# Block-causal attention and two feed-forward layers on one core: the first part as one list ordered at build time, with two-bank PSUM tiles and quartered tail scores

## The chip, the cores and the metric

The kernel runs on one core of a Trainium2 chip. The metric is the device time of one execution in microseconds, the lower the better. Before the change three runs gave 958.18, 959.80 and 960.07, a median of 959.8 us.

## The reference

Attention has 4 batches of 8 heads, 576 positions of 64 numbers, and a mask by blocks of 64: a query sees all keys of its own block and of earlier ones. Two feed-forward layers follow, each 512 to 2048 to 512 over 2304 tokens. All is float32.

```
scores = (q @ k.T) / sqrt(64);  scores = where(pos_q // 64 >= pos_k // 64, scores, -1e9)
attn   = exp(scores - max);  attn = attn / (sum(attn) + 1e-9);  x = attn @ v      # heads side by side
h = x @ w_in1;   g = where(h >= 1, h, where(h <= -1, 0, (h + 1)**2 / 4));  x = g @ w_out1
h = x @ w_in2;   g = h * cos(h);                                           out = g @ w_out2
```

## The kernel before

**Attention** goes over 16 pairs of heads (4 batches, 4 pairs each). The two heads of a pair lie in the upper and lower 64 partitions of `Q` and `K`. The 576 queries are four blocks of 128 and a tail of 64 (`LAST`, `TAIL`). For each pair: transposes bring K and Q from their loads (`prep`, L472; copies L478, L480, L485); score matmuls fill PSUM (`scores`, L505), the block scores of the two heads in two row halves of the array, with a short matmul `mk_k, mk_q` that adds the mask; VectorE takes the negated row maximum (L533), ScalarE the exponential with the row sum (L544), VectorE adds 1e-9 and takes the reciprocal (L562, L565; for tails L539, L553, L557), GpSimd multiplies (L573). `p_trans` transposes the probabilities (L600) and ScalarE or VectorE copies them out of PSUM (L616, L614); `pv` multiplies by V, the two heads in two column halves (L631), and ScalarE copies the result to `xs` (L642 to L645), which goes to DRAM (`x1d`).

The work of a pair has two groups, blocks 0, 1 and the tail (`GROUPS[0]`) and blocks 2, 3. The tail queries of both heads stand in one 128-column operand padded with zeros (`Q[:, S - TAIL:S + TAIL]`), so that a full-array matmul gives both heads' tail scores, the keys in two halves of 288; two half maxima, two half sums and two exponentials are joined afterwards. PSUM has eight tiles of one bank.

The order is a program's: `attention` yields after each piece, and `at(d, fn)` puts a follow-up (a reduce, an exponential, a copy) `d` pieces later. Weight conversion is called in the same way. A weight arrives as 64-bit words; ScalarE and GpSimd turn the two halves into fields (L267, L269, L273), VectorE joins them (L280, L284), and the float is rounded to a high part (L309 to L312) and a low rest (L251). Fourteen of the 32 halves of layer 1's weights are converted during attention, the others in layer 1.

**Layer 1** has 4.5 blocks of 512 tokens with 16 steps of 128 hidden columns. A step is `mm1` (12 matmuls, L755), the activation (L772, L775, L778, then L248 for the high part and L251 for the low part) and two steps later `mm2` (12 matmuls, L801). Each product is high by high, high by low and low by high. `first_split` splits the input of the first block while attention runs, right behind the scores of pairs 1 to 4. Layer 2's weights are combined during layer 1 (`w_combine`, L343 to L362) and stored to DRAM from GpSimd's queue (L374).

**Layer 2** (L970, L1062) is a seven-product scheme. Its operations stand in a list, `Plan`, which simulates four queues at build time with a cost for each operation and emits the instructions in that order.

The rule of `at`, and the calls that follow a score matmul:

```
at(1, top); at(2, exp)
if u == (3,) and 1 <= n <= NK: at(3, lambda: first_split(n - 1))
if u != (2,): at(5, norm)
```

Of the kernel before, what the change touches and what calls it, by code (L numbers as in the profile page):

```python
# [9 lines left out]
F32 = mybir.dt.float32  # L10
# [17 lines left out]

class Plan:

    def __init__(self):
        self.ops, self.wrote, self.read = [], {}, {}

    def add(self, eng, cost, reads, writes, fn):
        n, pre = len(self.ops), set()
        for r in reads:
            if r in self.wrote:
                pre.add(self.wrote[r])
            self.read.setdefault(r, []).append(n)
        for w in writes:  # L40
            pre.update(self.read.pop(w, ()))
            if w in self.wrote:
                pre.add(self.wrote[w])
            self.wrote[w] = n
        pre.discard(n)
        self.ops.append((eng, cost, pre, fn))

    def run(self):
# [3 lines left out]
        for i, (eng, cost, pre, fn) in enumerate(self.ops):  # L52
            for p in pre:
                post[p].append(i)
            if eng == "P":
# [4 lines left out]
        for i in reversed(range(n)):  # L60
            left[i] = self.ops[i][1] + max([left[j] + (0.0 if chain[j] == i else self.LAG) for j in post[i]], default=0.0)
        need = [len(op[2]) + (chain[i] is not None) for i, op in enumerate(self.ops)]
        ready_at, free = [0.0] * n, {"P": 0.0, "V": 0.0, "A": 0.0, "S": 0.0}
        ready = {e: [i for i in range(n) if self.ops[i][0] == e and need[i] == 0] for e in free}
        done = 0
        while done < n:
            best = None
            for e, r in ready.items():
                if r:
                    t = max(free[e], min(ready_at[i] for i in r))  # L70
                    if best is None or t < best[0]:
                        best = t, e
            t, e = best
            i = min((i for i in ready[e] if ready_at[i] <= t), key=lambda i: (-left[i], i))
            ready[e].remove(i)
            self.ops[i][3]()
            end = t + self.ops[i][1]
            free[e] = t if e == "S" else end
            for j in post[i]:
                need[j] -= 1  # L80
                ready_at[j] = max(ready_at[j], end + (0.0 if chain[j] == i else self.LAG))
                if need[j] == 0:
                    ready[self.ops[j][0]].append(j)
            done += 1

    LAG = 0.15
# [3 lines left out]
def attn_moe_moe_kernel(ctx: ExitStack, tc: tile.TileContext, q, k, v, w_in1, w_out1, w_in2, w_out2, out):  # L90
# [9 lines left out]
    NI = (S + 127) // 128  # L100
    TAIL = S - 128 * (NI - 1)
    LAST = NI - 1
    scale = 1.0 / float(D) ** 0.5

    const = ctx.enter_context(tc.tile_pool(name="const", bufs=1))
    dram = ctx.enter_context(tc.tile_pool(name="dram", bufs=1, space=DRAM))
    KB = 1024
# [32 lines left out]


# [14 lines left out]
    def warm():  # L156

        z = M.e.tile([128, 512], F32, name="warm", tag="ea")[:, 0:64]
        nc.vector.memset(z, 0.0)
        M.z = z.bitcast(BF16)  # L160
        M.zo = M.h[0].tile([128, 512], F32, name="h", tag="h")
        idle(36)

    def idle(n):
        for _ in range(n):
            tc.keep_in_program_order(nc.tensor.matmul(  # L166
                out=M.zo[:, 0:128], lhsT=M.z, rhs=M.z, start=True, stop=True, skip_group_check=True
            ))

    def consts():  # L170
        make_identity(nc, ident)

# [16 lines left out]


    now = [0]
    due = {}

    def at(d, fn):
        if d == 0:
            fn()
        else:
            due.setdefault(now[0] + d, []).append(fn)

    def tick():  # L200
        now[0] += 1
        for fn in due.pop(now[0], ()):
            fn()

    def flush():
        while due:
            tick()

    class Pools:
        pass  # L210

    M = Pools()
    M.wb = None
    M.two = []


    w_raw, w_in, w_out, rnds, raw_slot = {}, {}, {}, {}, {}
    srcs = {1: (w_in1, w_out1), 2: (w_in2, w_out2)}

    def home(f, which):  # L220
        arena, n = (M.A1, f) if f < NWA else (M.W2, f - NWA)
        return Slots(arena, (2 * n + which) * 4 * KB, 4 * KB)

    def w_load(layer, f, which):

        def load(slot, f):
            a = slot.tile([128, 2 * DM], I32)
            w = srcs[layer][which].bitcast(I32)
            if which == 0:
                dst = a.rearrange("p (k f) -> p k f", k=NK)  # L230
                src = w[:, f * 256:(f + 1) * 256].rearrange("(k p) f -> p k f", p=128)
            else:
                dst, src = a, w[f * 128:(f + 1) * 128, :]
            with tc.issue_after(P.loaded.ins):
                nc.sync.dma_start(out=dst, in_=src)
            return a

        if layer == 1:
            raw_slot[f, which] = M.raws.pop(0)
            w_raw[layer, f, which] = load(raw_slot[f, which], f)  # L240
        else:
            assert M.two.pop()
            w_raw[layer, f, which] = [
                load(Slots(M.F1, (8 + 4 * i) * KB, 4 * KB), f + NF // 2 * i) for i in range(2)
            ]

    def rounded(hi, raw):
        return nc.gpsimd.tensor_scalar(out=hi, in0=raw, scalar1=1.0, scalar2=1.0, op0=ALU.mult, op1=ALU.mult)  # L248

# [3 lines left out]
    def wait_for(i, other):  # L253
        tc.add_manual_dep(
# [1040 lines left out]
```

## Time and profile before

| | |
|---|---|
| median of 3 runs | 959.8 us (958.18 to 960.07) |
| profiled execution | 959.37 us, of which the span of the trace is 957.5 us |
| granted TensorE clock | 0.996 of full speed in the mean |
| busy | TensorE 943.0 us (98%), VectorE 703.3 (73%), ScalarE 542.2 (57%), GpSimd 349.2 (36%) |
| chain that ended last | TensorE 76%, VectorE 10%, ScalarE 8%, issue 2%, GpSimd 2%, DMA 1% |

In the trace PE is TensorE's matmuls and PEld its weight loads, DVE is VectorE, ACT ScalarE, POOL GpSimd, SP the queue that issues DMAs. Ends of matmuls are modelled, so that neighbours overlap; the distance from one start to the next is safer than a duration. A float32 matmul leaves two records. A row of busy time by stage has the stretch, its length, then busy time and instructions of PE, PEld, DVE, ACT and POOL, then the granted clock, DMA's share and GB/s. A row of a group of instructions has engine, operation, shapes and count, then busy time and the mean of one in ns, then the idle time in front of it and who ended it. A row of a timeline or of the chain has its start and its length in us.

### The profile page before, as it was taken

To read this page: it belongs to the slowest core of one execution; us is meant where nothing else is said; L and a number is where in the kernel's file an instruction comes from. 1 tells how busy PE (TensorE), PEld (TensorE's weight loads), DVE (VectorE), ACT (ScalarE), POOL (GpSimd) and SP (SyncE) were. 2 spreads that over 40 slices of the span, in tenths; PEclk is the share of its full clock that TensorE was granted. 3 is DMA by queue.
4 is the path that set the end of the run, shared out by engine and by line. 5 is a ranking of instruction groups with operands and counts; after the bars stand their busy time and mean duration, and the time that the engine had idled before them with its cause. 6 is when DMAs were issued, how large, how long until landed. Compare 5 with 4: busy or idle time off the path is not lost.

```text
span 957.5 us, 17583 instructions
## 1 busy us (share of the span) xinstructions
PE 943.0 (98%) x6524; PEld 843.4 (88%) x6524; DVE 703.3 (73%) x1078; ACT 542.2 (57%) x1067; POOL 349.2 (36%) x437
## 2 busy tenths in 40 slices
PE   8999999999999999999999999999999999999997
PEld 7777888778888888988888888999999999999997
DVE  5788887776766576787687622899977899578883
ACT  5778888865555555554455322568515684166641
POOL 2567776777755656576666110000000000000000
PEclk9999999999999999999999999999999999999999
DMA  5656555345347456646456450877798777877771
GB/s 113 188 146 162 158 146 144 94 157 185 101 144 252 155 190 238 205 176 226 170 180 242 140 190 19 268 253 252 258 311 300 253 245 260 276 275 252 250 261 52
DMA packets 131588, 188.84 MB, mean 197 GB/s; under 512 B 63408, under 2 KB 96688, under 8 KB 131504
## 3 DMA queue, kind: packets, MB, share of 16 engines
q1 hardware_dynamic: 123824, 158.36, 51.4%
q0 software_dynamic: 7680, 29.36, 8.3%
q8 instruction: 52, 0.85, 0.4%
q14 instruction: 32, 0.26, 0.1%
HBM read 144.18 MB, written 43.52 MB: 196 GB/s over the span
## 4 chain that ended last, share of the span: by engine, by line
PE 76%; DVE 10%; ACT 8%; issue 2%; POOL 2%; DMA 1%; SPq 0%; ACTq 0%; DVEq 0%; POOLq 0%
PE q L1062 19%; PE a L801 18%; PE q L970 18%; PE h L755 18%; ACT P L544 7%; DVE m L533 2%; DVE f L284 1%; DVE d L562 1%; DVE f L280 1%; DVE PT L614 1%; POOL m L251 1%; DVE g L251 1%; PE s L505 1%; DVE f L343 1%; PE h L166 1%
## 5 line engine op out<-in xcount | busy, mean ns | idle before, releaser
L1062 PE MATMUL q<-m 128*128 128x256 f32 x1512 | 181.9, 283 | 0.0
L1062 PEld LDWEIGHTS q<-m 128*128 128x128 f32 x1512 | 181.8, 192 | 0.0
L970 PE MATMUL q<-m 128*128 128x384 f32 x1008 | 175.2, 334 | 0.0
L970 PEld LDWEIGHTS q<-m 128*128 128x128 f32 x1008 | 174.7, 188 | 0.1
L801 PE MATMUL a<-g,m 128*128 128x512 f32 (+1 forms) x780 | 172.3, 368 | 1.3 <-DVE g L251 1.3
L801 PEld LDWEIGHTS a<-g,m 128*128 128x128 f32 x780 | 136.9, 188 | 26.9 <-DVE g L251 2.6
L251 DVE TENSOR_TENSOR g<-f,g 128x512 fp32r<-128x512 f32 (+1 forms) x80 | 70.8, 885 | 54.8 <-POOL g L248 54.7
L573 POOL TENSOR_SCALAR P<-P,r 128x576 f32<-128x576 f32 (+2 forms) x144 | 91.5, 652 | 51.1 <-DVE r L565 32.0
L544 ACT ACTIVATE P<-s,m 128x288 f32<-128x288 f32 (+4 forms) x160 | 81.4, 524 | 36.5 <-DVE m L539 28.1
L755 PE MATMUL h<-m 128*128 128x512 f32 (+1 forms) x468 | 98.7, 359 | 0.0
L772 ACT ACTIVATE f<-h,half 128x512 f32<-128x512 f32 (+1 forms) x80 | 51.2, 640 | 81.5 <-PE h L755 73.3
L248 POOL TENSOR_SCALAR g<-f 128x512 fp32r<-128x512 f32 (+1 forms) x80 | 54.9, 687 | 109.0 <-DVE f L778 104.3
L755 PEld LDWEIGHTS h<-m 128*128 128x128 f32 x468 | 79.0, 191 | 13.3 <-issue 0.8
L778 DVE SCALAR_TENSOR_TENSOR f<-f,h 128x512 f32<-128x512 f32 (+1 forms) x80 | 50.3, 628 | 49.9 <-ACT f L775 49.9
L755 PE MATMUL h<-x,m 128*128 128x512 f32 x312 | 75.9, 389 | 0.0
L533 DVE TENSOR_REDUCE m<-s 128x1 f32<-128x288 f32 (+4 forms) x160 | 67.2, 473 | 3.4 <-PE s L505 3.4
L505 PE MATMUL s<-K,Q 128*128 128x288 f32 (+4 forms) x320 | 67.6, 469 | 1.5 <-ACT P L544 1.2
L755 PEld LDWEIGHTS h<-x,m 128*128 128x128 f32 x312 | 58.3, 188 | 11.9
L280 DVE SCALAR_TENSOR_TENSOR f<-f 128x512 uint32<-128x512 uint32 x64 | 45.1, 725 | 19.4 <-ACT f L273 10.5
L631 PEld LDWEIGHTS s<-PT,rv 128*64 128x64 f32 x960 | 45.4, 137 | 14.1 <-ACT PT L616 8.9
L631 PE MATMUL s<-PT,rv 128*64 128x128 f32 (+1 forms) x960 | 52.4, 260 | 2.3 <-ACT PT L616 2.3
L939 ACT ACTIVATE f<-f,hpi 128x768 f32<-128x768 f32 x48 | 44.6, 929 | 16.2 <-DVE f L935 16.2
(121 smaller groups left out, 1506.4 us busy)
## 6 DMA issues: line engine op xcount, KB each, us to landing
m<-w2i SPq DMA_DIRECT2D x84, 512.0 KB, 4.2
m<-w2o SPq DMA_DIRECT2D x84, 512.0 KB, 3.6
f<-in_moe_w_in_dram SPq DMA_DIRECT2D x32, 512.0 KB, 4.7
f<-in_moe_w_out_dram SPq DMA_DIRECT2D x32, 512.0 KB, 4.1
w2i<-f POOLq DMA_DIRECT2D x8, 1024.0 KB, 5.3
w2o<-f POOLq DMA_DIRECT2D x8, 1024.0 KB, 4.7
w2i<-o POOLq DMA_DIRECT2D x8, 768.0 KB, 4.1
w2o<-o POOLq DMA_DIRECT2D x8, 768.0 KB, 4.0
```

What stands on the lines that cost most here:

```text
L248: return nc.gpsimd.tensor_scalar(out=hi, in0=raw, scalar1=1.0, scalar2=1.0, op0=ALU.mult, op1=ALU.mult)
L251: return (eng or nc.vector).tensor_tensor(out=lo, in0=raw, in1=hi.bitcast(F32), op=ALU.subtract)
L280: nc.vector.scalar_tensor_tensor(out=low.bitcast(U32), in0=top.bitcast(U32), scalar=0x80000000, in1=low.bitcast(U32), op0=ALU.bitwise_and, ...
L505: mm = lambda o, l, r, **kw: pin(nc.tensor.matmul(out=o, lhsT=l, rhs=r, skip_group_check=True, **kw))
L533: i = P.top = nc.vector.tensor_reduce(out=m[:, c:c + 1], in_=o, axis=AX.X, op=ALU.max, negate=True)
L544: P.act = nc.scalar.activation(out=pr[:, a:b], in_=o, func=ACTF.Exp, bias=m[:, e:e + 1], accum_out=den[:, c:c + 1],)
L573: P.div = nc.gpsimd.tensor_scalar(out=pr[:, a:b], in0=pr[:, a:b], scalar1=r[:, e:e + 1], scalar2=1.0, op0=ALU.mult, op1=ALU.mult,)
L631: pin(nc.tensor.matmul(out=ps[64 * h:64 * h + 64, c0:c0 + nq], lhsT=V[:, j, h, :], rhs=PT[:, a:a + nq], start=(j == 0), stop=(j == i), ski ...
L755: nc.tensor.matmul(out=hps[s][:, 0:n_], lhsT=w[:, a, kk * 128:(kk + 1) * 128], rhs=x[:, b], start=(kk == 0 and n == 0), stop=(kk == NK - 1 ...
L801: nc.tensor.matmul(out=o, lhsT=w[:, a, dm:dm + 128], rhs=b, start=(f == 0 and n == 0 and c == 0), stop=(f == NF - 1 and n == 2), skip_grou ...
L970: pin(nc.tensor.matmul(out=ps[:, e, 0:HT], lhsT=w[:, e, a, 128 * kk:128 * (kk + 1)], rhs=L2.xq[i][:, kk, c], start=(not src and kk == 0 an ...
L1062: pin(nc.tensor.matmul(out=ps[:, m // 2, 256 * (m % 2):256 * (m % 2) + 256], lhsT=t[:, e, a, 128 * m:128 * (m + 1)], rhs=w[:, e, o], start ...
```

## The change

Attention, weight conversion, layer 1 and the combining of layer 2's weights are now one `Plan`. Each operation names what it reads and writes, its cost on each engine that may run it (`A` ScalarE, `V` VectorE, `G` GpSimd), whether it holds a port that VectorE and GpSimd share (`lock`), and a latency for DMAs. TensorE's operations keep the order in which they are added; for attention this is a fixed list of units over two pairs, `PERIOD`. All other queues are ordered by the simulation, and copies and splits go to the engine that it finds free. Nothing is put a fixed number of pieces later any more.

```
 class Plan:
-    LAG = 0.15
+    LAG = 0.22
-    def add(self, eng, cost, reads, writes, fn):
+    def add(self, eng, cost, reads, writes, fn, lock=(), latency=0.0):
...
+    def cp(engines, n, out, in_, reads, writes, scale=1.0):
+        do(engines, costs(n, engines), reads, writes, lambda e: pin(copy(e, out(), in_(), scale)))
+    def diff(engines, n, lo, raw, hi, reads, writes):
+        c = {"V": 0.07 + n / 960.0, "G": 0.15 + 0.0022 * n}
+        do(engines, {e: c[e] for e in engines}, reads, writes,
+           lambda e: pin(rest(lo(), raw(), hi(), nc.gpsimd if e == "G" else nc.vector)), lock="GV")
...
+    PERIOD = (
+        ("T0", -2), ("T2", -2), ("S2", -1), ("S0", -1), ("PV", -2), ("pk", 0), ("pq", 1), ("Tb", -2),
...
+    EARLY, FROM_PAIR, PACE = 14, 1, (1, 1)
+    SWITCH, LEAD, KEEP = 0.07, 3, 4
```

In a unit's name S is scores, T transposes of probabilities, pk and pq the transposes of K and Q, PV the product with V, tl tail scores, Pt the tails' product; 3, 2 and 0 are block 3, block 2 and blocks 0 and 1 together, a and b the tails of the two pairs.

PSUM now has four tiles of two banks, named `t0` to `t3`, and each unit takes one (tail scores two). The planner picks the tile by an estimate of when it is free. One reduce covers both heads of a block, one copy a whole unit.

```
-        P.ps = [(stack.enter_context(tc.tile_pool(name="ps_s", bufs=4, space=PSUM, side="right")), "s")]
-        P.ps = (P.ps + [(M.h[0], "h")]) * 4
+    def ps_take(cost, hold, allowed=range(4)):
+        i = min(allowed, key=lambda i: (BANKS[i], i))
...
+            tiles[n] = M.ps[i // 2].tile([128, 2, 512], F32, name=f"t{i}", tag=f"t{i}")
...
+            do("V", 0.07 + 2 * nk / 960.0, [key], sk(0, n, 2 * x, 2 * x + 2), lambda e, x=x, off=off, nk=nk: pin(
+                nc.vector.tensor_reduce(
+                    out=stat(0, n, 2 * x, 2 * x + 2), in_=ps_of(r, i)[:, :, off:off + nk], axis=AX.X, op=ALU.max,
+                    negate=True,
+                )))
```

The tail queries of two pairs are scored together. Each of the four heads uses a quarter of the array, 64 rows by 64 columns; the zero padding goes. One reduce and one exponential cover a pair's tails.

```
-                    if tail:
-                        done[h] = mm(o, Q[:, S - TAIL:S + TAIL], K[:, HALF * h:HALF * (h + 1)], start=True, stop=True)
+            for a in range(2):
+                for x in range(2):
+                    for h in range(2):
+                        m = n + x
+                        o = 64 * (h if x == 0 else 1 - h)
+                        hd = slice(64 * h, 64 * h + 64)
+                        pin(nc.tensor.matmul(
+                            out=ps[x][o:o + 64, a, 0:HALF], lhsT=M.Q[m % 2][hd, S - TAIL:S],
+                            rhs=M.K[m % 2][hd, HALF * a:HALF * (a + 1)], start=True, stop=True, skip_group_check=True,
+                        ))
```

Fourteen weight halves are still converted in attention, one a pair from pair 1 on. K and Q loads have two buffers each. The stores of layer 2's combined weights go from GpSimd's queue to SP's, and layer 2's first inputs and weights are fetched by operations of the same list. `second`, which builds layer 2, keeps its operations; its `Plan` has the old lag of 0.15.

```
-            nc.gpsimd.dma_start(out=dst, in_=t.rearrange("p i a b -> p i (a b)").bitcast(F32))
+            dma(256 * n, [x for part in range(2) for x in tk(0, n, part)], [("wd", which, g, i)],
+                lambda: nc.sync.dma_start(out=dst, in_=t(0, n).rearrange("p i a b -> p i (a b)").bitcast(F32)))
...
-        plan = Plan()
+        plan = Plan(0.15)
```

How the order moves is seen at two places. First TensorE in the middle of attention, before: eleven transposes of probabilities, the tail scores of one pair (288 columns, from the padded operand), then blocks 0 and 1 of the same pair, then PV of another.

```order
L600 MATMUL s<-ident,P 128x128 x11
L505 MATMUL s<-K_179,Q_178 128x288 x2
L505 MATMUL s<-K_179,Q_178 128x128 x2
L505 LDWEIGHTS mk_q
L505 MATMUL s<-mk_k,mk_q 128x64
L505 LDWEIGHTS mk_q
L505 MATMUL s<-mk_k,mk_q 128x64
L505 MATMUL s<-K_179,Q_178 128x256 x2
L505 LDWEIGHTS mk_q
L505 MATMUL s<-mk_k,mk_q 128x64
L505 LDWEIGHTS mk_q
L505 MATMUL s<-mk_k,mk_q 128x64
```

Now, once in two pairs (`rv_113` and `rv_114` are V of an even and an odd pair, `K_109` and `K_110` their keys, `n` holds probabilities and their transposes):

```order
L624 MATMUL t_1159<-n,rv_114 64x128 x20
L652 MATMUL t_1190<-n,rv_113 64x64 x10
L652 MATMUL t_1190<-n,rv_114 64x64 x10
L565 MATMUL t_1220<-K_109,Q_111 64x288 x2
L565 MATMUL t_1221<-K_110,Q_112 64x288 x2
L565 MATMUL t_1220<-K_109,Q_111 64x288 x2
L565 MATMUL t_1221<-K_110,Q_112 64x288 x2
L478 MATMUL t_1235<-ident,rq_117 128x96 x6
L607 MATMUL t_1248<-ident,n 128x128 x8
L498 MATMUL t_1265<-K_110,Q_112 128x512 x2
```

The tail scores of two pairs stand together behind the products of an earlier two, twenty block products of a pair in one unit, and a unit of Q transposes and one of P transposes come before the next score tile.

Second VectorE in the same stretch. Before, one pair: the two weight joins, two reduces of tails and their join, four reduces of blocks 0 and 1, the tails' sum and reciprocal, three pieces of Q, then the blocks' sum and reciprocal and a copy.

```order
L280 SCALAR_TENSOR_TENSOR f<-f 128x512
L284 SCALAR_TENSOR_TENSOR f<-f 128x512
L533 TENSOR_REDUCE m<-s 128x1 x2
L539 TENSOR_TENSOR m<-m 128x1
L533 TENSOR_REDUCE m<-s 128x1 x4
L553 SCALAR_TENSOR_TENSOR d<-d 128x1
L557 RECIPROCAL r<-d 128x1
L485 TENSOR_SCALAR Q_178<-s 128x224
L485 TENSOR_SCALAR Q_178<-s 64x64 x2
L562 TENSOR_SCALAR d<-d 128x4
L565 RECIPROCAL r<-d 128x4
L614 COPY PT<-s 128x512
```

Now, from the tails' reduces on (`sm` holds maxima, sums and reciprocals):

```order
L572 TENSOR_REDUCE sm<-t_1220 128x1
L572 TENSOR_REDUCE sm<-t_1221 128x1
L206 COPY n<-t_1248 128x1024
L541 TENSOR_SCALAR sm<-sm 128x1
L512 TENSOR_REDUCE sm<-t_1265 128x2
L541 TENSOR_SCALAR sm<-sm 128x1
L545 RECIPROCAL sm<-sm 128x1
L308 SCALAR_TENSOR_TENSOR f<-f 128x512
L545 RECIPROCAL sm<-sm 128x1
L512 TENSOR_REDUCE sm<-t_1294 128x2
L512 TENSOR_REDUCE sm<-t_1306 128x2
L541 TENSOR_SCALAR sm<-sm 128x2
```

Reduces and copies are fewer and longer, the joins of a weight no longer stand next to each other, and the sums and reciprocals of a block come in three places instead of two.

## Rows read from the trace of the kernel before

**Rows 1.** Busy time by stage, the even pairs of attention

```profile
87.06:175.75 88.69, 88.69 (x1001) 73.47 (x1000) 73.62 (x201) 75.15 (x248) 66.95 (x97) 1.00 0.56 149
```

**Rows 2.** The chain that ended last, attention: start, length, what

```profile
63.19 2.01 ACT P L544 x7
...
75.98 2.01 ACT P L544 x7
...
175.75 2.45 ACT P L544 x7
```

**Rows 3.** Timeline of TensorE over one pair, unit by unit

```profile
109.43 1.75 PE L631 MATMUL s<-PT,rv 128*64 128x128 f32 x28
111.11 0.71 PE L472 MATMUL s<-ident,rk 96*128 96x96 f32 x6
111.66 1.37 PE L600 MATMUL s<-ident,P 128*128 128x128 f32 x11
112.86 1.56 PE L505 MATMUL s<-K,Q 128*128 128x288 f32 x8
...
114.92 1.46 PE L631 MATMUL s<-PT,rv 128*64 128x128 f32 x32
116.31 0.71 PE L472 MATMUL s<-ident,rq 96*128 96x96 f32 x6
116.86 1.69 PE L600 MATMUL s<-ident,P 128*128 128x128 f32 x14
118.48 1.09 PE L505 MATMUL s<-K,Q 64*128 64x384 f32 x4
```

**Rows 4.** Timeline of the weight loads, same pair and its end

```profile
113.93 0.30 PEld L505 LDWEIGHTS s<-K,Q 64*128 64x128 f32 x4 [0.39 <-ACT PT L616]
...
120.50 1.51 PEld L631 LDWEIGHTS s<-PT,rv 128*64 128x64 f32 x28 [0.45 <-ACT PT L616]
```

**Rows 5.** Groups by shape, TensorE, 112.8 to 114.2 us: one pair's tails

```profile
L505 PE MATMUL s<-K,Q 128*128 128x288 f32 x4 | 1.1, 406 | 0.0
```

**Rows 6.** Groups by shape, VectorE, 87.06 to 175.75 us

```profile
L284 DVE SCALAR_TENSOR_TENSOR f<-f 128x512 uint32<-128x512 uint32 x8 | 7.0, 874 | 0.3
L562 DVE TENSOR_SCALAR d<-d 128x4 f32<-128x4 f32 x16 | 6.0, 374 | 11.9 <-ACT P L544 11.9
...
L280 DVE SCALAR_TENSOR_TENSOR f<-f 128x512 uint32<-128x512 uint32 x8 | 5.5, 685 | 0.0
...
L565 DVE RECIPROCAL r<-d 128x4 f32<-128x4 f32 x16 | 2.8, 173 | 0.3
```

**Rows 7.** Timeline, GpSimd and VectorE at two places of attention

```profile
47.61 1.27 POOL L251 TENSOR_TENSOR m<-f,m 128x512 fp32r<-128x512 f32 x1
47.69 1.22 DVE L562 TENSOR_SCALAR d<-d 128x4 f32<-128x4 f32 x1 [0.51 <-ACT P L544]
...
119.69 2.21 DVE L533 TENSOR_REDUCE m<-s 128x1 f32<-128x384 f32 x4
```

**Rows 8.** Timeline of TensorE: attention's first scores, layer 1's first matmuls

```profile
8.27 1.66 PE L505 MATMUL s<-K,Q 128*128 128x288 f32 x8
...
192.06 4.36 PE L755 MATMUL h<-m 128*128 128x512 f32 x12
```

**Rows 9.** Groups, TensorE, 192 to 227 us: attention's last records

```profile
L631 PE MATMUL s<-PT,rv 128*64 128x128 f32 (+1 forms) x58 | 4.1, 266 | 0.0
L600 PE MATMUL s<-ident,P 128*128 128x128 f32 x14 | 2.0, 272 | 0.0
```

**Rows 10.** The chain that ended last, layer 1 and the beginning of layer 2

```profile
254.66 2.72 PE h L755 x12
...
384.45 1.44 PE a L801 x12
...
596.48 58.26 PE q L970 x336
```

More of the change, by code (lines that the diff above doesn't have):

```diff
@@ L60, in run @@
         for i in reversed(range(n)):
[L61 to L66, printed above, removed]
+            costs, _, _, _, latency = self.ops[i]
@@ new lines, in run @@
+            left[i] = min(costs.values()) + latency + max(
+                [left[j] + (0.0 if chain[j] == i else self.lag) for j in post[i]], default=0.0)
+        need = [len(op[1]) + (chain[i] is not None) for i, op in enumerate(self.ops)]
+        ready_at, free, port = [0.0] * n, {e: 0.0 for e in "PVAGS"}, 0.0
+        ready = {e: set() for e in free}
+        for i in range(n):
+            if need[i] == 0:
+                for e in self.ops[i][0]:
+                    ready[e].add(i)
+        for _ in range(n):
@@ L79, in run @@
+            t, (_, cost, i), e = best
+            costs, _, fn, lock, latency = self.ops[i]
+            for o in costs:
+                ready[o].discard(i)
+            fn(e)
+            end = t + cost
+            free[e] = end
+            if e in lock:
+                port = end
             for j in post[i]:
                 need[j] -= 1
-                ready_at[j] = max(ready_at[j], end + (0.0 if chain[j] == i else self.LAG))
+                ready_at[j] = max(ready_at[j], end + latency + (0.0 if chain[j] == i else self.lag))
@@ L82, in run @@
                 if need[j] == 0:
[L83 to L86 removed]
+                    for o in self.ops[j][0]:
+                        ready[o].add(j)
+            if self.trace is not None:
+                self.trace.append((t, cost, e, i))
+    trace = None
 @with_exitstack
@@ L220, in home @@
[L220 to L245, printed above, removed]
@@ new lines, in dma, with span, w_home @@
+    def dma(kb, reads, writes, fn):
+        do("S", 0.1 + kb / 230.0, reads, writes, lambda e: fn(), latency=2.0)
+    def span(name, off, size):
+        return [(name, b) for b in range(off // 512, (off + size + 511) // 512)]
+    M.A1 = Arena("m", 88)
+    M.A2 = Arena("n", 32, F32)
+    M.G = Arena("g", 12)
+    M.F1 = Arena("f", 24, F32)
+    NW1, NW2 = 9, 4
+    X1 = 72
+    def w_home(f, which):
+        arena, n = ("m", f) if f < NW1 else ("n", f - NW1) if f < NW1 + NW2 else ("w", f - NW1 - NW2)
+        off = (2 * n + which) * 4 * KB
+        return arena, off
@@ L259, in parts, with x_keys @@
+    def x_keys(half, kk, part=None):
+        arena, off = x_home(half, kk)
+        return span(arena, off, 4 * KB) if part is None else span(arena, off + 2 * KB * part, 2 * KB)
+    raw_n, v_n = [0], [0]
     def parts(raw):
@@ new lines, in idle, with x_load @@
+    def idle(n, t):
+        for _ in range(n):
+            pin(nc.tensor.matmul(
+                out=t[:, 0, 0:128], lhsT=M.z, rhs=M.z, start=True, stop=True, skip_group_check=True
+            ))
+    halves = [tuple(range(j, min(j + 2, NBLK))) for j in range(0, NBLK, 2)]
+    blocks = halves[:2] + halves[4:] + halves[2:4]
+    steps = [(kb, f) for kb in range(len(blocks)) for f in range(NF)]
+    nsteps = len(steps)
+    hps, accs = {}, {}
+    def x_load(kb):
+        x_half, js = 1 - kb % 2, blocks[kb]
```

1242 lines of the change are left out of this document (597 added, 645 removed), and 2 rows, old and new, of the table PERIOD.

## The prediction

> **What bounds the kernel now.** I read the page first, then the busy time by stage, then the chain of waits, then the timeline of one pair. The page has TensorE busy 98% of the span, which says little, since ends of matmuls are modelled. The stages say more. In the even part of the attention [rows 1] TensorE reads 88.69 of 88.69 us, VectorE 73.62, ScalarE 75.15 and GpSimd 66.95: nothing is idle for long, and no other engine is full. The chain of waits [rows 2] runs there through ScalarE's exponentials and VectorE's small statistics, not through matmuls, and its marks show the beat: one pair takes 75.98 - 63.19 = 12.79 us among the first pairs and (175.75 - 75.98) / 9 = 11.09 us afterwards. So the attention is held by the hand-offs between in-order queues, with TensorE close behind.
>
> How close, the timeline of one pair shows [rows 3], start to start, the last start being in [rows 4]: PV of the two big blocks 1.68, K transposes 0.55, eleven P transposes 1.20, tail scores with blocks 0 and 1 2.06, PV of the small blocks 1.39, Q transposes 0.55, fourteen P transposes 1.62, scores of blocks 2 and 3 2.02. Sum 11.07, the whole beat. Two known waits are in it, both for ScalarE's copies out of PSUM: 0.39 us in front of the block scores and 0.45 us in front of PV [rows 4].
>
> The attention as a whole holds TensorE from 8.27 to 192.06 [rows 8], 183.8 us, and 58 PV records and 14 transposes lie later among layer 1 [rows 9]. At the rates of [rows 3] (60 PV records in 1.68 + 1.39, 14 transposes in 1.62) these are 3.0 + 1.6 = 4.6 us, so 188.4 us in all.
>
> Layer 1 is different: twelve 512-column matmuls take 2.72 us, twelve of 256 columns 1.44 [rows 10]. Its 1536 wide and 384 narrow ones need 348.2 + 46.1 = 394.3 us. From 192.06 to 596.48 are 404.4 us; less the 4.6 of attention, 399.8: only 5.5 us are lost there. Layer 2 then runs from 596.48 without a gap [rows 10]; its operations and the rules that order them stay, and I price it at nothing changed. It is hidden by no one: it is TensorE's own work.
>
> **The change, part by part.**
>
> *Tail scores in quarters.* Now each pair multiplies its zero-padded tail queries over the full array: four records of 288 columns, 1.1 us of TensorE [rows 5]. Afterwards two pairs share the array, eight matmuls of 64 rows and 64 columns for two pairs. If four run at once, two pairs cost what one costs now: 0.55 us a pair saved, 8.8 us over 16 pairs. Nothing in this trace runs in quarters; the nearest rows are the two row halves of the block scores and the two column halves of PV, which do run together. Bounds: four at once, 1.1 us for two pairs; one at a time, 8 x 0.55 = 4.4 us. I take four at once, by those nearest rows, and keep the other end for a rival. The exponential and the sum that join two half-tails go as well (one 576-wide exponential for two of 288); ScalarE and VectorE gain below half a microsecond a pair, which is counted in VectorE's sum below.
>
> A rule of the Trainium skill speaks against it: TensorEngine Tiling (Array Packing), section Restrictions and Gotchas, says that different row tiles cannot access one PSUM bank at the same time. Here the two heads of a pair use different row halves and write the same bank, though its upper and lower partitions. By the rule the quarters would take turns; no run here shows it.
>
> *One list, ordered at build time.* TensorE's order becomes a fixed period of two pairs, the same instructions apart from the tails. Without the two waits and with the cheaper tails a pair needs 11.07 - 0.39 - 0.45 - 0.55 = 9.7 us; with the waits, 10.5. Which of them stays is decided by VectorE. In two pairs of the new order it has 10 reduces over 6272 elements a lane, 9 copies out of PSUM over 5184, 4 integer joins, 8 tensor_scalar and 8 reciprocals. Four reduces over 1792 elements take 2.21 us back to back [rows 7], 1.23 ns an element; at that price for reduces and copies 7.7 + 6.4 us. Joins 2 x (0.685 + 0.874) = 3.1, reciprocals 8 x 0.173 = 1.4 [rows 6]. The tensor_scalar reads 0.374 in the mean [rows 6], but is four elements wide: where GpSimd holds a 1.27 us subtraction it lasts 1.22 [rows 7]. At the mean, 3.0 us; at the reciprocal's price, 1.4. Sum 20.0 to 21.6, that is 10.0 to 10.8 us a pair, above TensorE's 9.7.
>
> The Trainium skill has this as an exclusive lock (SBUF — State Buffer, section Who interferes with whom): a tensor_scalar may take the port pair that VectorE shares with GpSimd, and who comes second waits for the whole instruction. The 1.22 beside 1.27 agrees. By the rule the eight would be worth up to 8 x 1.27 us in two pairs, by the mean 3.0.
>
> So I take 10.6 us a pair, near VectorE's middle, and TensorE waits about 0.9 us of it. The 12.79 us of the early pairs goes: there the first four blocks of layer 1's input are split on the chain; in the new list this is one VectorE and one ScalarE or GpSimd instruction a pair, beside other work. Over 16 pairs 169.6 us. For the beginning and the end of the pipeline I add 3.5 us: the first pair's softmax must end before its first transposes (about 1.2), the four splits (0.6 each on VectorE, half of it covered, 1.2), the last pair's softmax, behind which layer 1's first three steps are put (1). In all 173.1 against 188.4: a gain of 15.3 us.
>
> *Two-bank PSUM tiles.* Four tiles instead of eight one-bank tiles. A tile is held while it is filled and read out. Filling by the units of [rows 3], 1.23 ns an element for reduces and copies, four exponentials over 1792 elements in 2.45 us [rows 2] and some 0.2 us a hand-off give, for the 23 tiles of two pairs, 24 us for scores and tails, 14 for P transposes, 13 for the rest and 4 of hand-offs: an estimate of 55 us out of 4 x 21.2 = 85. I price it at nothing: the cover is 30 us. Were each of the eight score and tail tiles held 3.7 us longer, in a queue in front of the exponentials, it would be gone.
>
> *Weights.* Fourteen conversions during attention, as now, and eighteen after it; their low parts may run on VectorE or GpSimd, and the stores of layer 2's weights move from GpSimd's queue to SP's. SP then has them among raw loads, attention's loads and stores and layer 1's inputs; a store waits for its split, and the next raw load queues behind it, which has the time of a step (5.4 us) and more. Layer 1's loss of 5.5 us can at most vanish and may come back, since VectorE's combinations meet the half-size block again. I take 4.0 left: a gain of 1.5; bounds +5.5 and -5.
>
> **Sum.** The profiled execution took 959.37 us (span 957.5, 1.9 outside); the median of the runs shown is 959.8, so the base differs by 0.4. 959.4 - 15.3 - 1.5 = 942.6 us.
>
> **Rivals.**
> *The list does what it can.* VectorE's long instructions cost less than 1.23 ns an element, because their fixed part is paid once, and the beat comes near TensorE's floor, 9.9 us. 158.4 + 2.5 = 160.9 for attention, gain 27.5; layer 1 loses 2, gain 3.5; 928.4 us. For it: the floor is 9.7. Against: VectorE's sum.
> *VectorE becomes the bound.* The tensor_scalar wait for GpSimd as the worst row shows, joins stay at 0.87, and the beat is 11.1 us. 177.6 + 4.5 = 182.1, gain 6.3, layer 1 unchanged: 953.1 us. For it: VectorE at 10.8 by the upper price, and queues that are in order. Against: in the even pairs it reads only 83% now [rows 1].
> *The quarters take turns* (slower). If the eight tail matmuls run one at a time they take 4.4 us for two pairs, 1.65 us a pair more than forecast, and TensorE is the bound: a beat of 12.25, 196 + 3.5 = 199.5, a loss of 11.1, less 1.5 from layer 1: 969.0 us. It decides against the change from a beat of (188.4 - 3.5) / 16 = 11.6 on, that is when two pairs' tails take over 3.1 us. Two at a time (2.2 us) only bring the beat to 11.15, the case before.
>
> **How the numbers follow.** Forecast 0.50, with a range of its own of 936 to 949; the floor 0.20; VectorE bound 0.20; quarters in turn 0.10. A measurement of this kernel tells 0.2%, some 2 us, from no change. Faster: 0.50 + 0.20 + nearly all of the 0.20, so 0.89; within 0.2%: 0.02, the edge of the VectorE case; slower 0.09. The range takes the floor at its middle and the VectorE case whole: 928 to 957 us; what lies outside is half of the floor's chance and the quarters'.
>
> **What would show it.** In the profile of the changed kernel: tail scores of two pairs, from the first of eight records' group to the next unit, in 1.0 to 1.3 us (4.4 would be the third rival); marks of the chain two pairs apart by 20.5 to 22 us, the first ones too; layer 1's first matmul near 177 instead of 192; layer 2's first near 580 instead of 596.5, and its length 356 us again. TensorE's longest waits in attention on VectorE's or ScalarE's copies. Wrong would be: waits for a score tile's release by the exponentials, a beat over 11.5, a gap in front of layer 2 for weights that SP brought late, or a layer 1 that loses more than 10 us.

## The result, and the profile after

The kernel after takes **934.25 us** (median; 933.22 to 935.05) against 959.11 for the kernel before: a ratio of 0.974, 95% interval 0.9723 to 0.9757. The forecast was 942.6. The gain is 24.9 us where 16.8 were forecast. Its profiled execution has a span of 933.3 us against 957.5, 24.2 less.

First the busy time by stage in the even part, the answer to [rows 1]: window, length, and the busy us (instructions) of TensorE, its weight loads, VectorE, ScalarE and GpSimd; then granted clock, DMA share and GB/s.

```profile
57.00:78.00 21.00, 21.00 (x266) 16.80 (x270) 18.28 (x39) 18.12 (x52) 13.41 (x22) 1.00 0.68 173
...
99.00:120.00 21.00, 21.00 (x268) 16.61 (x258) 18.64 (x43) 17.83 (x50) 13.61 (x22) 1.00 0.64 168
...
sum 84.00, PE 84.00 PEld 66.99 DVE 73.99 ACT 71.56 POOL 54.20; mean PE 21.00 PEld 16.75 DVE 18.50 ACT 17.89 POOL 13.55
```

TensorE has no gap here, and before it had none between 87.06 and 175.75 us [rows 1]. VectorE is at 88% now (73.99 of 84.00), where it was at 83%. The page's chain, which ran through ScalarE and VectorE in attention [rows 2], is now TensorE's own work:

```profile
PE 96%; DVE 1%; DMA 1%; ACT 1%; issue 0%; SPq 0%; ACTq 0%
```

The timeline of TensorE over one period of two pairs answers to [rows 3]. A unit's time is its start to the next unit's start.

```profile
118.99 1.22 PE L565 MATMUL t<-K,Q 64*64 64x288 f32 x16
120.14 0.71 PE L478 MATMUL t<-ident,rq 96*128 96x96 f32 x6
120.69 1.04 PE L607 MATMUL t<-ident,n 128*128 128x128 f32 x8
121.66 1.13 PE L498 MATMUL t<-K,Q 64*128 64x512 f32 x4
...
125.97 2.40 PE L624 MATMUL t<-n,rv 128*64 128x128 f32 x40
128.30 0.71 PE L478 MATMUL t<-ident,rk 96*128 96x96 f32 x6
...
136.20 2.40 PE L624 MATMUL t<-n,rv 128*64 128x128 f32 x40
138.44 1.33 PE L652 MATMUL t<-n,rv 128*64 128x64 f32 x40
139.70 0.70 PE L565 MATMUL t<-K,Q 64*64 64x288 f32 x5
```

The tail scores of two pairs take 1.15 us, about what one pair took before [rows 5]. The period is 139.70 - 118.99 = 20.71 us, 10.35 a pair. The marks of L565 (36.21, 56.90, 77.58, 98.29, 118.99, 139.70) stand 20.70 apart from 36.21 us on, so the slow early pairs of [rows 2] are gone.

The ends of the stages, from TensorE's timeline and then from the chain, answer to [rows 8] and [rows 10]:

```profile
8.27 1.13 PE L498 MATMUL t<-K,Q 64*128 64x512 f32 x4
...
170.40 1.72 PE L607 MATMUL t<-ident,n 128*128 128x128 f32 x14 [0.38 <-DVE xs L206]
171.88 1.63 PE L723 MATMUL h<-m 128*128 128x512 f32 x6
```

```profile
264.73 2.73 PE h L723 x12
...
383.86 1.44 PE h L723 x12
...
572.40 58.26 PE q L906 x336
```

Attention is 171.88 - 8.27 = 163.6 us, and its four late pieces among layer 1 are 4.86 us by their starts: 168.5 where it was 188.4. Layer 1 is 572.40 - 171.88 - 4.86 = 395.7 us where it was 399.8, for 394.3 of matmuls. Layer 2 begins 24.1 us earlier and is as long as it was. So 19.9 us come from attention and 4.1 from layer 1.

The 19.9 can be split by the marks. The beat is 11.09 - 10.35 = 0.74 us shorter, 11.8 us over 16 pairs, of which the quarters are 0.48 a pair (e10 below), 7.7 us. Three early pairs took 12.79 us instead of 11.09 (the marks of L544 at 37.60 and 50.40 belong to them besides those of [rows 2]), 5.1 us. The other 3.0 are the two ends. No run has the old order with the new tiles, so what of the rest is the list's and what the two-bank tiles' stays open.

VectorE's groups by shape, 57 to 141 us, answer to [rows 6]; behind them two neighbours in its timeline.

```profile
L512 DVE TENSOR_REDUCE sm<-t 128x2 f32<-128x1024 f32 x8 | 9.8, 1220 | 3.9 <-PE t L498 3.9
...
L315 DVE SCALAR_TENSOR_TENSOR f<-f 128x512 uint32<-128x512 uint32 x8 | 5.4, 680 | 0.0
L308 DVE SCALAR_TENSOR_TENSOR f<-f 128x512 uint32<-128x512 uint32 x7 | 4.8, 679 | 0.0
L541 DVE TENSOR_SCALAR sm<-sm 128x2 f32<-128x2 f32 x17 | 4.5, 265 | 0.3
```

```profile
102.20 0.14 DVE L541 TENSOR_SCALAR sm<-sm 128x1 f32<-128x1 f32 x1
102.27 1.21 DVE L512 TENSOR_REDUCE sm<-t 128x2 f32<-128x1024 f32 x1
```

Both joins take 0.68 us now, where one took 0.87. The durations of all twenty groups of that stretch add up to 84.3 us, but VectorE was busy for 73.99: the next instruction starts before the last has ended, as the two rows show (102.27 lies inside the one from 102.20). One period of 20.70 us holds 84.3 x 20.70 / 84 = 20.8 us of durations and 18.2 us of busy time.

### The profile page after: what moved, and what is told of

The parts are those of the page before. It is cut to its first block, busy times and chain, and to the rows that moved or that the text cites. A ratio compares the mean times of both kernels' runs of the same rounds, so it can differ in the third digit from the quotient of the medians.

```text
span 933.3 us, 17355 instructions
## 1 busy us (share of the span) xinstructions
PE 924.8 (99%) x6572; PEld 829.4 (89%) x6572; DVE 691.7 (74%) x1050; ACT 577.2 (62%) x1032; POOL 159.9 (17%) x240
## 4 chain that ended last, share of the span: by engine, by line
PE 96%; DVE 1%; DMA 1%; ACT 1%; issue 0%; SPq 0%; ACTq 0%
PE h L723 21%; PE a L764 21%; PE q L998 19%; PE q L906 19%; PE t L607 4%; PE t L498 4%; PE t L624 4%; PE t L478 2%; PE t L652 1%; PE t L565 1%; DMA rq<-in_q_dram 1%; PE t L670 1%; ACT n L524 0%; DVE sm L512 0%; DVE n L206 0%
## 5 line engine op out<-in xcount | busy, mean ns | idle before, releaser
L906 PEld LDWEIGHTS q<-m 128*128 128x128 f32 x1008 | 174.7, 188 | 0.1
L998 PE MATMUL q<-m,n 128*128 128x256 f32 x1260 | 153.8, 283 | 0.0
L998 PEld LDWEIGHTS q<-m,n 128*128 128x128 f32 x1260 | 152.4, 192 | 0.0
L764 PE MATMUL a<-g,m 128*128 128x512 f32 (+1 forms) x540 | 118.5, 368 | 0.1
L549 POOL TENSOR_SCALAR n<-n,sm 128x256 f32<-128x256 f32 (+3 forms) x144 | 83.0, 594 | 45.3 <-DVE sm L545 30.2
L524 ACT ACTIVATE n<-t,sm 128x512 f32<-128x512 f32 (+3 forms) x128 | 65.7, 539 | 7.7 <-DVE sm L512 7.7
L512 DVE TENSOR_REDUCE sm<-t 128x2 f32<-128x1024 f32 (+2 forms) x64 | 50.3, 819 | 14.6 <-PE t L498 14.6
L764 PE MATMUL a<-g,n 128*128 128x512 f32 (+1 forms) x240 | 52.5, 368 | 0.0
L607 PE MATMUL t<-ident,n 128*128 128x128 f32 x400 | 51.6, 275 | 0.4 <-DVE xs L206 0.4
L607 PEld LDWEIGHTS t<-ident,n 128*128 128x128 f32 x400 | 43.6, 141 | 8.5 <-POOL n L549 5.0
```

What stands on the lines that cost most here:

```text
L512: nc.vector.tensor_reduce(out=stat(0, n, 2 * x, 2 * x + 2), in_=ps_of(r, i)[:, :, off:off + nk], axis=AX.X, op=ALU.max, negate=True,)))
L524: pin(nc.scalar.activation(out=P, in_=ps_of(r, i)[:, h, off:off + nk], func=ACTF.Exp, bias=stat(0, n, e0, e0 + 1), accum_out=stat(1, n, e0 ...
L549: do("G", 0.26 + 0.0008 * nk, sk(2, n, e0, e0 + 1) + [key], [key], lambda e: pin(nc.gpsimd.tensor_scalar(out=P(), in0=P(), scalar1=stat(2, ...
L607: pin(nc.tensor.transpose(ps[:, 128 * j:128 * (j + 1)], P[:, a:a + 128], ident))
L764: pin(nc.tensor.matmul(out=o, lhsT=wt[:, a, dm:dm + 128], rhs=b, start=(f == 0 and i == 0 and c == 0), stop=(f == NF - 1 and i == 2), skip ...
L906: pin(nc.tensor.matmul(out=ps[:, e, 0:HT], lhsT=w[:, e, a, 128 * kk:128 * (kk + 1)], rhs=L2.xq[i][:, kk, c], start=(not src and kk == 0 an ...
```

## The experiments

The theory after the result: TensorE's own work sets the beat (20.70 us for two pairs), and the list, its priorities and four tiles are what lets the other engines keep up. The rival: VectorE at 88% sets it, and TensorE only reads full, since its ends are modelled. All differences below are to 934.25 us; the kernel after, run again beside the last experiment, gave 934.05 (933.57 to 934.38). The kernel before, run beside each group of experiments, had medians of 958.9 to 959.2.

| run | median us | ratio to before | 95% interval |
|---|---|---|---|
| e1_quarter_order | 934.03 | 0.9743 | 0.9714 to 0.9771 |
| e2_three_tiles | 955.92 | 0.9972 | 0.9953 to 0.9991 |
| e3_no_priority | 956.94 | 0.9981 | 0.9969 to 0.9992 |
| e4_reduce_twice | 944.79 | 0.9855 | 0.9826 to 0.9884 |
| e5_no_port | 950.38 | 0.9910 | 0.9896 to 0.9925 |
| e6_tails_twice | 942.72 | 0.9826 | 0.9809 to 0.9842 |
| e7_reduce_left_out | 934.04 | 0.9748 | 0.9720 to 0.9775 |
| e8_reordered | 934.80 | 0.9752 | 0.9737 to 0.9767 |
| e9_more_switches | 940.46 | 0.9802 | 0.9786 to 0.9818 |
| e10_two_quarters | 939.68 | 0.9796 | 0.9781 to 0.9811 |
| e11_hoisted | 933.71 | 0.9738 | 0.9724 to 0.9751 |

### TensorE or VectorE: e6, e7, e4

**e6_tails_twice** gives TensorE more to do and nobody else.

```diff
-            for a in range(2):
+            for a in (0, 1, 0, 1):
...
-        tensor(1.0, [(t, c) for t in "KQ" for c in range(2)], ...
+        tensor(2.1, [(t, c) for t in "KQ" for c in range(2)], ...
```

> The sixteen tail-score matmuls in quarters of two pairs are issued twice (the planner counts 2.1 us for them): TensorE alone does about 1.0 us more per two pairs, 8 us in all; PSUM tiles, VectorE and ScalarE do what they did. Theory A (TensorE is the bound of the beat): 940 to 944 us. Rival B (VectorE or the tiles are the bound and TensorE only looks full): under 937 us.

It took 942.72 us, +8.5: all of the added work arrives. (The tail scores of two pairs are eight matmuls; the trace has sixteen records of them.) Its tail unit in TensorE's timeline is 2.12 us, 0.97 more than after, 7.8 us over eight units, and its later marks stand 21.68 apart, 0.98 more:

```profile
102.08 2.19 PE L565 MATMUL t<-K,Q 64*64 64x288 f32 x32
104.20 0.71 PE L478 MATMUL t<-ident,rq 96*128 96x96 f32 x6
```

**e7_reduce_left_out** takes work from VectorE and leaves TensorE's.

```diff
-        for x, off in subs:
+        for x, off in subs if u != 2 else ():
             nk = 128 * (x + 1)
             do("V", 0.07 + 2 * nk / 960.0, ...
...
+                m0 = 6 + h if u == 2 else e0
...
-                        bias=stat(0, n, e0, e0 + 1), ...
+                        bias=stat(0, n, m0, m0 + 1), ...
```

> Block 2's row maxima are not taken; its exponentials use those of block 3 as bias (so the softmax of block 2 is shifted by other numbers than the reference's). VectorE does 0.95 us less per pair, 15 us in all, and TensorE what it did. Theory A (with TensorE at the bound, VectorE just under it): 930 to 934.5 us. Rival B (VectorE is the bound): at least 0.6 us per pair comes back, under 925 us.

934.04 us: nothing comes back. The busy times over the stretch of the first fence, four windows together, show VectorE relieved by 9.2 us and TensorE as full as it was:

```profile
sum 84.00, PE 84.00 PEld 67.13 DVE 64.84 ACT 71.42 POOL 57.85; mean PE 21.00 PEld 16.78 DVE 16.21 ACT 17.86 POOL 14.46
```

**e4_reduce_twice** goes the other way: block 2's reduce is issued twice.

```diff
+            for _ in range(2 if x == 2 else 1):
                 do("V", 0.07 + 2 * nk / 960.0, ...
```

> The row maximum of block 2 is taken twice, 0.95 us more of VectorE in every pair, known to the planner; VectorE then reads about 10.2 of 10.35 us a pair. Theory A (TensorE is the bound and VectorE is only cover, 1.1 us a pair of it): at most 4 us more, 934 to 938. Rival B (as the prediction had it, VectorE holds the beat): 0.95 x 16 = 15 us more, about 949.

944.79 us, +10.5 of the 15.2 added. The busy time between its marks at 58.89 and 146.10 us, eight pairs, and TensorE's longest wait there:

```profile
58.89:146.10 87.21, 85.26 (x1036) 66.31 (x1032) 77.84 (x168) 68.35 (x187) 55.53 (x89) 1.00 0.63 158
```

```profile
PE t L478 <- ACT n L525: 1.1, 3, 0.5
```

A pair takes 10.90 us there, 0.55 of the added 0.95 more, with VectorE busy for 89% of the stretch; the rest of the 10.5 lies at the two ends and in layer 1. So the rival's 0.95 a pair does not come out, but neither does the theory's forecast (934 to 938): far less is free on VectorE's side than its 12% of idle time suggests. Whether it is VectorE's own time that runs out is not shown, since block 2's score tile is held 0.95 us longer too, and the wait above is for an exponential that reads a tile. e6 and e7 settle the question between the two engines: TensorE is the bound of the beat.

### The quarters: e1, e10

**e1_quarter_order** exchanges the loops of the tail matmuls, so that the two of one quarter stand next to each other.

```diff
-            for a in range(2):
-                for x in range(2):
-                    for h in range(2):
+            for x in range(2):
+                for h in range(2):
+                    for a in range(2):
```

> The same eight tail matmuls of two pairs, but both key halves of one quarter of the array directly behind each other, so that a quarter blocks the queue for its own second matmul. Theory A (quarters run four at once, and TensorE is now the bound of all of attention): the tail unit grows from 1.15 us to about 2.4 (five slots of 0.48, since only the second of one quarter runs beside the first of the next), 1.25 us more in each of 8 units, and all of it arrives: about 944 us. Rival B (the quarters already take turns, or TensorE has slack): the unit stays or the 10 us are absorbed, 934 to 936 us.

934.03 us, and the tail unit takes 1.15 to 1.16 us as before the exchange. The idea that a matmul waiting for its own quarter holds up the others behind it fell. That the quarters take turns, the run's other reading, is excluded by the next one.

**e10_two_quarters** puts both pairs' tails into the same two quarters, one behind the other.

```diff
-                        o = 64 * (h if x == 0 else 1 - h)
+                        o = 64 * h
...
-        tensor(1.0, [(t, c) for t in "KQ" for c in range(2)], ...
+        tensor(2.0, [(t, c) for t in "KQ" for c in range(2)], ...
```

> The second pair's tail scores go to the same two array quarters as the first pair's (rows and columns of the head's own half), and the P V product of the tails reads them there; everything else as after the change, with 2.0 us counted for the unit by the planner. Theory A (the four quarters work side by side, and TensorE sets the beat): the unit takes 2.1 us in place of 1.15, 0.9 to 1.0 us per two pairs, 7 to 8 us in all: 941 to 943 us. Rival B (the quarters take turns by pairs in any case): no change, 933 to 936 us.

TensorE's timeline has 2.09 us for the unit, and the marks stand 21.65 apart (99.87, 121.52), 0.95 more than after:

```profile
99.87 2.16 PE L565 MATMUL t<-K,Q 64*64 64x288 f32 x16
101.96 0.71 PE L478 MATMUL t<-ident,rq 96*128 96x96 f32 x6
...
121.52 1.67 PE L565 MATMUL t<-K,Q 64*64 64x288 f32 x12
```

So four quarters do work side by side, 1.15 us where two take 2.09. The time, 939.68 us, is only 5.4 above after, less than the 7 to 8 expected: the list of this kernel also begins better, its second tail unit standing at 34.79 us where after has 36.21. Seven full periods at 0.95 less that 1.4 are 5.2.

### The list: e2, e3, e5

**e2_three_tiles** takes one of the four PSUM tiles away.

```diff
-        i = min(allowed, key=lambda i: (BANKS[i], i))
+        i = min([i for i in allowed if i != 1], key=lambda i: (BANKS[i], i))
```

> Three two-bank PSUM tiles in attention instead of four. Theory A (the estimate of the prediction: two pairs hold about 55 us of tile time, which is two thirds of four tiles at a beat of 20.7, but nine tenths of three): TensorE begins to wait for releases, 4 to 15 us more, 938 to 949. Rival B (tiles are held much shorter than estimated): 934 to 936. Rival C (four tiles are nearly full already): over 30 us more.

955.92 us, +21.7, between the first theory's 15 and the third's 30. What the first one describes happens, waits for releases, but at more than its size. Marks of L565 stand 23.3 to 23.8 us apart (62.07, 85.38, 109.16, 132.47, 155.78). What TensorE waited for from the first scores to layer 1, in us, times and the longest one:

```profile
PE t L624 <- ACT n L524: 4.1, 8, 1.8
PE t L607 <- POOL f L298: 3.3, 4, 0.8
PE t L498 <- ACT n L201: 2.9, 9, 0.4
PE t L607 <- ACT Q L201: 2.6, 3, 0.9
```

The first, third and fourth row are waits for an instruction that reads a PSUM tile, an exponential or a copy; the second, for GpSimd's weight fields, is not.

**e3_no_priority** orders the list by the order of writing instead of by the length of the chain behind an operation.

```diff
-            left[i] = min(costs.values()) + latency + max(...)
+            left[i] = float(n - i) if self.lag > 0.2 else min(costs.values()) + latency + max(...)
```

> The planner of the first part still simulates times, but among operations ready at once it takes the one that was added first instead of the one with the longest way to the end. Theory A (TensorE's fixed order of units and the simulated times do the work, the other queues have cover of about a tenth): at most 5 us more, below 940. Rival B (the priority is what keeps VectorE and ScalarE from holding TensorE up): waits return in attention and layer 1 falls behind with weights in its queue, 15 us or more, above 949.

956.94 us, +22.7. The marks of L565 from 57.00 to 145.96 are 22.1 to 22.5 apart, and layer 1's first matmul stands at 182.76, 10.9 late. TensorE's longest waits from 150 us on are two in layer 1 and one of 2.22 us just in front of it, at 180.49:

```profile
PE a L764 <- DVE g L197: 6.7, 2, 5.2
PE t L607 <- DVE xs L206: 2.2, 1, 2.2
```

So the second theory holds: waits return, and layer 1 waits for VectorE. A part is TensorE's clock: behind the wait of 5.25 us that ends at 232.28 the granted clock is 0.58 from 232 to 234 us, and eleven 512-column matmuls took 4.22 us, where at 2.4 GHz twelve take 2.72 [rows 10].

**e5_no_port** drops the lock between VectorE and GpSimd from the list's reckoning.

```diff
-                    t = max(free[e], ready_at[i], port if e in self.ops[i][3] else 0.0)
+                    t = max(free[e], ready_at[i])
```

> The planner no longer lets the joins and the writes of fp32r low parts wait for GpSimd's products (the lock on the port between VectorE and GpSimd is not counted when the list is ordered); all operations stay. Theory A: the order that the port rule gives is why the joins and the short tensor_scalar are shorter than before (0.68 us and 0.26 us against 0.87 and 0.37), so without it they meet GpSimd's products again: some 0.4 to 0.7 us of VectorE per pair, of which what is above 0.3 arrives: 936 to 940 us, and the mean of the two joins is above 0.75 us. Rival B: the list keeps them apart in any case, since GpSimd is little used: 933 to 935 us with joins as they are.

950.38 us, +16.1, more than either theory said. VectorE's groups, 57 to 141 us, and TensorE's waits after 150 us:

```profile
L308 DVE SCALAR_TENSOR_TENSOR f<-f 128x512 uint32<-128x512 uint32 x8 | 8.1, 1012 | 1.2 <-ACT f L293 1.2
...
L315 DVE SCALAR_TENSOR_TENSOR f<-f 128x512 uint32<-128x512 uint32 x8 | 6.5, 807 | 0.3
...
L541 DVE TENSOR_SCALAR sm<-sm 128x2 f32<-128x2 f32 x15 | 4.9, 329 | 2.6 <-ACT n L524 2.5
```

```profile
PE a L764 <- DVE o L206: 5.3, 1, 5.3
```

The joins meet GpSimd again (1.01 and 0.81 us in the mean against 0.68; one from 94.25 us took 1.55, beside a GpSimd subtraction of 1.27 from 93.98), and attention is 5.6 us longer (layer 1 starts at 177.49). The list is ordered anew as well, so that not all of the 5.6 need be the joins'. The rest is not attention's: one wait of 5.30 us between two blocks of layer 1, and behind it TensorE runs slowly. The granted clock by stretch:

```profile
280.00:287.00 7.00, 1.70 (x7) 0.88 (x6) 4.00 (x7) 3.75 (x7) 0.92 (x1) 0.90 0.74 244
287.00:290.00 3.00, 3.00 (x8) 2.32 (x8) 2.13 (x4) 2.52 (x4) 0.39 (x1) 0.50 0.95 317
...
295.00:300.00 5.00, 5.00 (x24) 4.14 (x23) 2.05 (x4) 1.51 (x4) 2.93 (x3) 1.00 0.00 1
```

After standing still for 5.30 us it was granted 1.2 GHz, and eighteen 512-column matmuls took 6.86 us, where they take 4.08 at 2.4 GHz: another 2.8 us. That makes 13.7 of the 16.1; the last 2.4 were not located. The Trainium skill (SBUF — State Buffer, Who interferes with whom) has a VectorE instruction with two SBUF inputs contend with a GpSimd instruction that reads SBUF; the joins have two such inputs, and 0.68 against 1.01 us, with the 1.55 beside 1.27, agrees.

### What is left on TensorE: e9, e8, e11

**e9_more_switches** has the same units with 15 changes of TensorE's kind of tile in two pairs instead of 11.

```diff
-        ("T0", -2), ("T2", -2), ("S2", -1), ("S0", -1), ("PV", -2), ("pk", 0), ("pq", 1), ("Tb", -2),
-        ("T3", -1), ("pk", 1), ("T2", -1), ("S3", 0), ("Ta", -2), ("T0", -1), ("S0", 0), ("S2", 0),
+        ("T0", -2), ("T2", -2), ("S2", -1), ("pk", 0), ("S0", -1), ("PV", -2), ("pq", 1), ("Tb", -2),
+        ("T3", -1), ("T2", -1), ("S3", 0), ("Ta", -2), ("T0", -1), ("S0", 0), ("pk", 1), ("S2", 0),
```

> The same units; the two preparations of K in a period are moved into the middle of two score runs, so that TensorE changes between kinds of tile (64*128, 128*64, 64*64, and 96*128 or 128*128) 15 times in two pairs, where it was 11. Theory A (each change costs about 0.17 us of TensorE's time, as the start-to-start times of the units in the trace after the change suggest, and TensorE sets the beat): 4 more changes, 0.7 us per two pairs, 5 to 6 us in all: 938.5 to 941 us. Rival B (a change costs no more than the 0.07 us that the planner counts, or nothing): 934 to 936.5 us.

940.46 us, +6.2, about as the first theory has it, but only part of it for that reason. The L565 rows of its TensorE timeline show periods of two lengths, 21.26 us (from 101.00) and 22.18 (from 78.82):

```profile
78.82 1.50 PE L565 MATMUL t<-K,Q 64*64 64x288 f32 x16
...
101.00 1.20 PE L565 MATMUL t<-K,Q 64*64 64x288 f32 x16
...
122.26 1.50 PE L565 MATMUL t<-K,Q 64*64 64x288 f32 x16
```

The short one has no wait in the timeline; it is 0.56 longer than after's, 0.14 a change. The long one has waits besides (the unit of 1.50 us is 1.43 to the next start, not 1.15). The Trainium skill says without a figure that changing the tiling mode drains TensorE (TensorEngine Tiling (Array Packing), Key Properties); this agrees, at 0.14 us.

**e8_reordered** has another order of the period and unit times as measured after the change.

```diff
...
+    PERIOD = (('T2', -2), ('T0', -2), ('S2', -1), ('S0', -1), ('PV', -2), ('pq', 0), ('pq', 1), ('pk', 1),
+              ('Tb', -2), ('pk', 0), ('T3', -1), ('Ta', -2), ('T2', -1), ('S3', 0), ('T0', -1), ('S0', 0),
+              ('S2', 0), ('Pt', -2), ('PV', -1), ('tl', 0), ('T3', 0), ('S3', 1))
...
-    SWITCH, LEAD, KEEP = 0.07, 3, 4
+    SWITCH, LEAD, KEEP = 0.17, 3, 4
```

> The same units in another order of the period (still eleven changes of TensorE's tiling mode per two pairs; block 0's and 2's transposes exchanged, the four K and Q preparations in one stretch, the tails' P V product ahead of the last pair's), ordered with the unit times that the trace after the change shows (1.15 us for the tails' scores with its change of mode, 0.17 us per change). Theory A (the beat is set by TensorE's own work, so an order can only give back at the ramp and at the hand-over to layer 1): 930 to 933 us. Rival B (it does nothing that can be measured): 933 to 936 us. Above 937 would say that the order of the period is tuned to waits that the unit times don't show.

934.80 us: no gain, as the second theory had it. Layer 1 starts at 169.79, 2.1 us earlier, and loses it again at the change of blocks. Timeline of VectorE and TensorE there:

```profile
273.33 0.69 DVE L206 COPY o<-a 128x512 f32<-128x512 f32 x1 [3.40 <-DMA x2d<-o]
...
274.07 1.64 PE L764 MATMUL a<-g,m 128*128 128x512 f32 x6 [1.98 <-DVE o L206]
```

The accumulator's copy waits for a store that still reads the staging buffer. **e11_hoisted** has e8's order and puts 1.5 us of the next step's `mm1`, taken from its old place, in front of that matmul.

```diff
...
+            kb, f = steps[x - 2]
+            for part in range(2 * len(blocks[kb])):
+                if part == 2 and f == 0 and kb >= 1:
+                    mm1(steps[x + 1], (0, 1))
                 mm2(steps[x - 2], part)
```

> e8_reordered, whose trace reached layer 1 2.1 us earlier than the kernel after and lost 1.98 us in one wait at 274.07 us (the first matmul into accumulator part 2 of layer 1's second block waits for VectorE's copy of that accumulator, which waits for the store of part 0 to leave its staging buffer). Here the first half of the next layer-1 product stands between parts 1 and 2 of a block's first step, 1.5 us of TensorE's own work in place of that wait. Theory A (TensorE is the bound everywhere, so a wait filled with its own work is a gain): 932 to 933.5 us, 1 to 2 us under the kernel after. Rival B (the wait moves on, to the hoisted product's own buffers or to the next step): 934 to 935 us.

933.71 us (933.32 to 934.42) beside 934.05 for after: not to be told apart. The wait shrank from 1.98 to 1.08 us and did not go. No version tried beats the kernel after by more than a measurement can tell.

## Why the prediction was right, and where it was not

**The quarters** were forecast at 0.55 us a pair, four at once. Measured: two pairs' tails in 1.15 us instead of about 2.1, 0.48 a pair by e10. The rule from the Trainium skill (TensorEngine Tiling (Array Packing), Restrictions and Gotchas), by which row tiles cannot use one PSUM bank at the same time, did not hold them back: two heads' row halves write different partitions of a bank, and the unit still takes 1.15 us and not the 4.4 of the third rival.

**The beat** came out at 10.35 us for a forecast of 10.6, but that it came so near is luck: the step that gave 10.6 failed. I let VectorE set it, at 10.0 to 10.8, over a TensorE floor of 9.7, with TensorE waiting about 0.9 us a pair. Measured, TensorE sets it (e6, e7) and has no wait in the middle of attention, and both numbers were off:
- *TensorE's floor was too low.* I subtracted the two waits of [rows 4], 0.84 us a pair. They are waits of the weight loads, and matmuls in flight covered them: the tail scores begin at 112.86 [rows 3] and take 1.1 [rows 5], so they end at 113.96, and the load that had waited starts at 113.93. That TensorE reads 88.69 of 88.69 [rows 1] agrees with it. Without that subtraction the floor is 11.07 - 0.55 = 10.5, and 10.35 was measured; the last 0.2 was not taken apart.
- *VectorE's sum was too high.* The durations were about right (20.8 us for two pairs, forecast 20.0 to 21.6). But durations of neighbours overlap, and 18.2 us of busy time is what they fill.

**The early pairs** lost their 12.79 us beat, as forecast. **The ramps** were put at 3.5 and are 168.5 - 16 x 10.35 = 2.9. Attention thus gained 19.9 us instead of 15.3: 16 x 0.25 from the beat and 0.6 from the ramps make the difference of 4.6.

**Layer 1** was the term most mis-sized for its own size: 4.0 us left by the forecast, 1.4 measured. One reason stood in my own rows. In [rows 8] the first twelve 512-column matmuls read 4.36 us, and at 2.4 GHz such twelve take 2.72 [rows 10]. In the kernel before TensorE had just stood still for 2.33 us, and the granted clock of that stretch is 0.66 in the mean:

```profile
191.47 0.66 PE L631 MATMUL s<-PT,rv 128*64 128x128 f32 x4 [2.33 <-ACT PT L616]
```

```profile
190.00:195.00 5.00, 3.53 (x11) 2.64 (x12) 3.26 (x4) 3.03 (x7) 4.92 (x6) 0.66 0.51 169
```

From 192.06 to 196.26, the next unit's start, are 4.20 us: 1.5 lost to the lower clock. After the change the longest wait at that place is 0.38 us, and the granted clock reads 1.00 from 170 to 176 us. Three waits for VectorE in the kernel before (0.37, 0.19 and 0.76 us) are gone too; the last 1.3 of the 4.1 were not taken apart.

**The two-bank tiles** were priced at nothing, and from 36 us to the end of the full periods nothing in TensorE's timeline waits for one (in front of that, two waits of 0.53 and 0.80 us are for exponentials). But the cover I worked out, 30 of 85 us, was not there: with three tiles, 62 us at the measured beat for an estimated 55, two pairs take 2.6 to 3.1 us longer (e2). The likely reason, which no run shows by itself, is that a tile is held while its reader queues, which the sum of work times leaves out.

**The rivals.** The floor case (928.4) had the right bound with a floor that was too low, and for another reason than the one shown: VectorE's long instructions were not much cheaper (1.22 us for 1024 elements are 1.19 ns each, for 1.23), they overlap. The result lies between it and the forecast. VectorE as the bound is refuted by e7, quarters in turn by the 1.15 us. The sum of that last rival was wrong too: it added TensorE's 1.65 us to a beat of 10.6 that was VectorE's. From the prediction's own floor 9.7 + 1.65 = 11.35 follows, under the 11.6 from which it calls the change a loss. The range and the sign held.

## What to carry to other kernels

A weight load that waits is not a matmul unit that waits: before a wait is subtracted, see whether the matmuls ahead of it end later than the wait does. When an engine reads full without a gap, test it by doubling one of its units and by taking work from its rival; both answers together settle the bound in two runs. And a twelve-matmul row that lasts longer than its like in the same table is the clock or a stall, and belongs in the sum.

## What the runs showed of the hardware

- TensorE was granted 1.2 GHz after standing still for 2.33 us (before, up to 191.47; the granted clock is 0.50 from 193 to 194 us), for 2.22 us (e3, up to 180.49; 0.50 from 182 to 184) and for 5.30 us (e5); behind the last eighteen 512-column matmuls took 6.86 us instead of 4.08. Around the waits of 1.98 us (e8) and 1.08 us (e11) the stretch from 270 to 280 us reads 1.00.
- A change between kinds of tile costs TensorE 0.14 us (e9).
- Two 64 x 64 quarters of one row half and two of the other run together while writing the same banks in different partitions, in both orders of issue that were tried (1.15 us after and in e1, 2.09 for two quarters in e10).
- Durations of neighbouring VectorE instructions overlap: 84.3 us of them filled 73.99 us of busy time (after, 57 to 141 us).
- A VectorE join of 0.68 us took 1.55 beside a GpSimd subtraction (e5, at 94.25).
